# A gated linear recurrence and a gated MLP on one core: the recurrence cut into chunks of 64 tokens, its products as 64x64 blocks in four quadrants of TensorE

## The chip, the cores and the metric

The kernel runs on 1 core of one Trainium2 chip. The metric is the device time in microseconds (us) of one execution; lower is better. The engines of the core are named as in the profile: PE is TensorE (its weight loads are PEld), DVE is VectorE, ACT is ScalarE, POOL is GpSimd, SP is SyncE, which here issues all DMAs.

## What is computed

Two stages stand in a row. The first is a recurrence over 768 tokens for 4 sequences and 8 heads of 48 numbers, with a state of 48x48 per head that decays by a factor of its own for each token and row:

```python
for t in range(S):
    kt, vt, rt, wt = (k[:, :, t], v[:, :, t], r[:, :, t], w[:, :, t])
    cur = np.einsum('bhd,bhe->bhde', u[None] * kt, vt)
    y[:, :, t] = np.einsum('bhd,bhde->bhe', rt, state + cur)
    state = wt[:, :, :, None] * state + np.einsum('bhd,bhe->bhde', kt, vt)
```

The second takes y as x, 768 tokens of 384 numbers for each sequence:

```python
h = gelu_tanh(x @ w_in)                 # 384 -> 1024
u, v = h[..., :512], h[..., 512:]
v_n = (v - mean(v)) / sqrt(var(v) + 1e-6) * g_ln
v_s = einsum('ts,bsd->btd', w_sg, v_n) + b_sg    # over the tokens
out = x + (u * v_s) @ w_out             # 512 -> 384
```

## The kernel before

**The recurrence** is cut into steps of 128 tokens (`C`), 24 in all: 6 for each sequence. Heads stand in 4 pairs (`p`), one head of a pair in partitions 0 to 63 and the other in 64 to 127 (`j`). Within a step the recurrence becomes matrix products. A step has these parts, each a generator of its own:

- `decays` (line 403) makes running products of the decays with two scans on DVE (lines 408 and 413) and multiplies r by them (415); `decayed_k` does so for k (436).
- `own_weights` (439) makes one number per token and head, the term with `u`. For the first 8 steps (`OWN_PE`) PE sums it, with 4 matmuls of 8 columns (line 450); for the others three vector operations do (458, 460, 463). The numbers are put on the diagonal of two 128x512 blocks `a`, one for each `j`, by POOL (473) or by four ACT instructions (471).
- `scores` (477): 8 matmuls, one per head, give k against r over the step, 128x128 each (line 486, 64 rows of PE), and two `copy_predicated` (490) put what lies above the diagonal into `a`.
- `state` (492): 4 transposes of k (500), a copy, 8 matmuls with V (510), and an addition to the decayed state (520). `decayed` (522) multiplies the state by the decay of the step (531, 533). The last step of a sequence needs no new state and leaves this out.
- `outputs` (538): y is the product of the state with r (line 548, 8 matmuls; not in a sequence's first step) plus the product of `a` with V (line 563, 8 matmuls over 128 rows and 64 columns of PE). Three copies (267) carry y out of PSUM.

All these matmuls are float32. The profile lists two matmul records for each, and one for a transpose.

**The second stage** uses float32r operands split into a high and a low part, so that each product is three matmuls (lines 632, 633 and 634): `v_piece` (12 products of 512 columns for 128 tokens), `u_piece`, `gate_piece` and `out_piece` (products of 384 columns). They are called the dense matmuls here; there are 216 of 512 columns and 1152 of 384. x is split on PE for the first 6 steps (621, 622), later on DVE (627). Weights come as float64 bits and are turned into high and low parts on DVE and ACT; for `w_in` with PE's help (772, 773, 774).

**The order** is written ahead of the run by a planner (`Plan`). Each part yields operations with a cost on each engine that could do it, what it comes after and which buffers it takes; the planner keeps a clock for each engine, and where an operation may go on several engines it picks the one that ends it first. Ranks (`LEAD`, `FIRST`, `PIECE`, `WEIGHT`) say which stage goes first where two are ready. The instructions of each engine stand in the order that comes out; each engine keeps to it and waits at semaphores. The core's buffers for `a_ps` (2 banks for the scores), `k_ps` (transposed k, then the new state) and `y_ps` are one each in PSUM, and there are three `m_ps` for the second stage.

Of the kernel before, what the change touches and what calls it, by code (L numbers as in the profile page):

```python
# [12 lines left out]
U8 = mybir.dt.uint8  # L13
# [7 lines left out]
C = 128  # L21
NC = S // C
# [6 lines left out]
Q = C + 1  # L29
WL = NP * Q + 1  # L30
# [3 lines left out]
LEAD = (2.78, 2.05, 2.47, 2.9)  # L34
FIRST = {"v": -1.57, "u": 4.03, "gate": 5.24, "out": 7.56}
PIECE = {"v": -0.45, "u": 3.56, "gate": 5.0, "out": 7.56}
WEIGHT = {"v": -8.15, "u": -9.0, "sg0": 4.48, "sg1": 3.78, "out": 4.95, "g": -1.62}

OWN_PE = 8
COLD = 20.0  # L40
# [28 lines left out]
class Op:  # L69
# [3 lines left out]
    def __init__(self, on, after=(), take=(), free=(), done=None, kb=None, two=False):  # L73
        self.on, self.after, self.take, self.free, self.done, self.kb = on, after, take, free, done, kb
        self.two = two

# [29 lines left out]
class Slots:  # L106
# [5 lines left out]
    def since(self):  # L112
        return min(t for t, _ in self.free)
# [6 lines left out]
class Plan:  # L120
# [12 lines left out]
    @staticmethod  # L133
    def cost(e, c, t):
        return 2 * c if e == "PE" and t < COLD else c
# [13 lines left out]
    def run(self):  # L149
        while True:  # L150
            best = {}
            for p in self.procs:
# [3 lines left out]
                ready = max([p[2]] + [e.t for e in op.after] + [s.since() for s in op.take])  # L156
                t, c, e = min((s + self.cost(e, c, s), self.cost(e, c, s), e) for e, c in op.on.items()
                              for s in (max(ready, self.engines[e], self.port if op.port(e) else 0.0),))
                best.setdefault(e, []).append((t - c, p[0], p[4], p))
# [24 lines left out]
            p[2] = op.seen  # L184
# [75 lines left out]
def rwkv_gmlp(ctx: ExitStack, tc: tile.TileContext, wpad, kr, vtok, ktok, vt, u, w_in, g_ln, w_sgT, b_sg, w_out, out):  # L260
# [17 lines left out]
    ones = cp.tile([128, 128], F32, name="ones")  # L278
# [21 lines left out]
    s_w = slots("W", 2, [2 * 521])  # L300
# [18 lines left out]
    m_a = slots("a_ps", 1, [NP, C], [NP, C], at=ps)  # L319
# [6 lines left out]
    mask = per.tile([128, NP, C], U8, name="mask")  # L326
# [26 lines left out]
    plan.engines.update(DVE=2.0, POOL=3.0, ACT=2.1, SP=0.8)  # L353
# [23 lines left out]

    def load_kr(n):
# [3 lines left out]
        ch[n].kr.n = (g < NC - 1) + 1 + (g > 0)  # L382
# [3 lines left out]
    def load_v(n):  # L386
# [3 lines left out]
        ch[n].v.n = (g < NC - 1) + 1  # L390
# [9 lines left out]
    blocks = lambda t, o: t[:, o:o + NP * Q].rearrange("p (q x) -> p q x", x=Q)[:, :, 0:C]  # L400
    cols = lambda t: t.rearrange("p (q x) -> p q x", x=C)

    def decays(n):

        x = ch[n]
        yield Op({"DVE": 1.15}, after=[x.e_W], done=x.e_suf, two=True)
# [5 lines left out]
        yield Op({"DVE": 1.15}, done=x.e_pre, two=True)  # L412
# [5 lines left out]
    def range_check(n):  # L418
# [4 lines left out]
        both = x.w.tile.rearrange("p (a x) -> p a x", x=521)[:, :, 0:WL - 1]  # L423
        nc.scalar.activation(junk.rearrange("p (a x) -> p a x", a=2), both, AF.Square, accum_out=chk[:, n:n + 1])  # L424

    def chunk_pc(n):
        x = ch[n]
        op = yield Op({"ACT": 0.13, "POOL": 0.38}, after=[x.e_suf], take=[s_pc], done=x.e_pc)
        x.pc, = op.got
        x.w.done(op.seen)  # L430
        copy(op.e, x.pc.tile, x.Suf[:, 1:WL - 1:Q])
# [7 lines left out]
    def own_weights(n):  # L439

        x = ch[n]
        if n < OWN_PE:
# [4 lines left out]
            op = yield Op({"PE": 0.35}, after=[e_uc], take=[m_m], free=[rk])  # L447
# [16 lines left out]
        x.a = []  # L464
        for j in range(2):
            op = yield Op({"POOL": 0.95, "ACT": 1.2}, take=[s_a], done=(x.e_A0, x.e_A1)[j], free=[own] if j else [])
            x.a += op.got
            a = x.a[j].tile
            if op.e == "ACT":
                for p in range(NP):  # L470
                    nc.scalar.activation(a[:, p], ident, AF.Copy, scale=own.tile[:, 2 * p + j:2 * p + j + 1])  # L471
            else:
                nc.gpsimd.affine_select(a, own.tile[:, j:H:2].unsqueeze(2).broadcast_to([128, NP, C]),  # L473
# [594 lines left out]
```

## Time and profile before

| what | us |
|---|---|
| median of 3 runs (lowest, highest) | 403.65 (403.12, 405.01) |
| the profiled execution's own time | 402.04 |
| its span, first to last instruction | 400.3 |
| first PE instruction after the start | 6.39 |
| start of the last dense matmul | 393.51 |

The span is 1.74 us shorter than the profiled execution's time: this lies around the span. Durations in the profile are those of single instructions. Matmuls are pipelined, so that the busy time of one is longer than the distance from its start to the next start; what a group of matmuls costs on PE is read from the starts in the timeline. In a row of the timeline, "x16" is the number of records merged into it, "64\*64 64x128" the part of PE used (rows\*columns) and the moving operand. In a row of the windows, each engine has its busy time in that stretch and the number of its instructions that ran in it. The profile leaves out a few matmul records (1151 of 1152 are there).

### The profile page before, as it was taken

To read this page: it belongs to the slowest core of one execution; us is meant where nothing else is said; L and a number is where in the kernel's file an instruction comes from. 1 tells how busy PE (TensorE), PEld (TensorE's weight loads), DVE (VectorE), ACT (ScalarE), POOL (GpSimd) and SP (SyncE) were. 2 spreads that over 40 slices of the span, in tenths; PEclk is the share of its full clock that TensorE was granted. 3 is DMA by queue.
4 is the path that set the end of the run, shared out by engine and by line. 5 is a ranking of instruction groups with operands and counts; after the bars stand their busy time and mean duration, and the time that the engine had idled before them with its cause. 6 is when DMAs were issued, how large, how long until landed. Compare 5 with 4: busy or idle time off the path is not lost. (4 is left out here: it accounts for less than half of the span.)

```text
span 400.3 us, 7881 instructions
## 1 busy us (share of the span) xinstructions
PE 378.3 (95%) x2964; PEld 329.8 (82%) x2964; DVE 294.2 (73%) x573; ACT 200.2 (50%) x534; POOL 94.2 (24%) x127
## 2 busy tenths in 40 slices
PE   2799889999999999999999999999999999999993
PEld 2666567889898988988899988979899789999993
DVE  7699989889989999998798489956653355543251
ACT  3566575685555447746454246563272576502010
POOL 3003551123073543444550003124100002100000
PEclk9999899999999999999999999999999999999999
DMA  8918667343134634335422316222133520100101
GB/s 281 355 42 250 188 220 241 129 135 105 46 131 160 221 118 144 98 122 196 155 88 77 105 65 211 60 88 96 61 106 111 186 95 2 39 22 0 61 0 66
DMA packets 23933, 48.82 MB, mean 122 GB/s; under 512 B 4048, under 2 KB 13008, under 8 KB 23888
## 3 DMA queue, kind: packets, MB, share of 16 engines
q1 hardware_dynamic: 23888, 48.25, 36.6%
q8 instruction: 25, 0.41, 0.4%
q14 instruction: 20, 0.16, 0.1%
HBM read 42.34 MB, written 4.72 MB: 118 GB/s over the span
## 5 line engine op out<-in xcount | busy, mean ns | idle before, releaser
L632 PE MATMUL m_ps<-wsgh,vn 128*128 128x384 f32 x192 | 67.7, 353 | 0.8 <-DVE g L714 0.8
L634 PE MATMUL m_ps<-wsgh,vn 128*128 128x384 f32 x192 | 64.7, 337 | 0.0
L633 PE MATMUL m_ps<-wsgl,vn 128*128 128x384 f32 x192 | 64.6, 337 | 0.0
L473 POOL TENSOR_SCALAR_AFFINE_SELECT a<-own 128x512 f32<-128x512 f32 x25 | 20.3, 815 | 94.9 <-PE y_ps L563 44.9
L632 PEld LDWEIGHTS m_ps<-wsgh,vn 128*128 128x128 f32 x192 | 36.1, 188 | 5.5 <-issue 2.9
L712 ACT CAST g<-m_ps 128x384 fp32r<-128x384 f32 x32 | 15.1, 479 | 50.1 <-DVE m_ps L710 50.0
L490 DVE COPY_PREDICATED a<-mask,a_ps 128x512 f32<-128x512 uint8 x48 | 34.4, 730 | 4.5 <-POOL a L473 2.5
L663 POOL TENSOR_TENSOR st<-st,mhalf 128x1 f32<-128x1 f32 x24 | 15.3, 640 | 90.9 <-DVE st L661 87.7
L633 PEld LDWEIGHTS m_ps<-wsgl,vn 128*128 128x128 f32 x192 | 36.2, 188 | 0.4
L634 PEld LDWEIGHTS m_ps<-wsgh,vn 128*128 128x128 f32 x192 | 36.1, 188 | 0.0
L708 DVE SCALAR_TENSOR_TENSOR m_ps<-m_ps,g_ln,b_bc 128x384 f32<-128x384 f32 x32 | 19.7, 622 | 21.5 <-PE m_ps L634 21.4
L632 PE MATMUL m_ps<-g,wouth 128*128 128x384 f32 x96 | 33.7, 351 | 0.4 <-DVE g L714 0.4
L632 PE MATMUL m_ps<-xT,winh 128*128 128x384 f32 x96 | 33.4, 348 | 0.0
L408 DVE TENSOR_TENSOR_SCAN W<-W,D 128x516 f32<-128x516 f32 x24 | 32.0, 1332 | 1.6 <-DMA W<-in_wpad 1.6
L634 PE MATMUL m_ps<-xT,winl 128*128 128x384 f32 x96 | 32.4, 337 | 0.0
L633 PE MATMUL m_ps<-xT,winh 128*128 128x384 f32 x96 | 32.4, 337 | 0.0
L633 PE MATMUL m_ps<-g,wouth 128*128 128x384 f32 x96 | 32.4, 337 | 0.0
L634 PE MATMUL m_ps<-g,woutl 128*128 128x384 f32 x96 | 32.4, 337 | 0.0
L413 DVE TENSOR_TENSOR_SCAN W<-W,D 128x516 f32<-128x516 f32 x24 | 31.4, 1308 | 0.1
L471 ACT ACTIVATE a<-ident,own 128x128 f32<-128x128 f32 x92 | 29.1, 393 | 3.9 <-DVE own L463 3.8
L632 PE MATMUL m_ps<-winh,xT 128*128 128x512 f32 x72 | 30.5, 424 | 0.0
L424 ACT ACTIVATE junk<-W 128x1032 f32<-128x1032 f32 x24 | 25.6, 1066 | 9.8 <-DVE W L413 6.8
(142 smaller groups left out, 856.5 us busy)
## 6 DMA issues: line engine op xcount, KB each, us to landing
KR<-in_kr SPq DMA_DIRECT2D x24, 512.0 KB, 3.5
W<-in_wpad SPq DMA_DIRECT2D x24, 258.5 KB, 2.9
RK<-in_ktok SPq DMA_DIRECT2D x16, 384.0 KB, 3.2
vtok<-in_vtok SPq DMA_DIRECT2D x24, 192.0 KB, 3.1
out<-o SPq DMA_DIRECT2D x24, 192.0 KB, 1.9
KR<-in_w_in SPq DMA_DIRECT2D x6, 512.0 KB, 4.1
u<-in_w_sgT SPq DMA_DIRECT2D x12, 192.0 KB, 3.6
vn<-in_w_in SPq DMA_DIRECT2D x3, 512.0 KB, 7.3
```

Source lines behind the costliest of these rows:

```text
L408: nc.vector.tensor_tensor_scan(Suf[:, WL - 1:0:-1], W[:, WL - 1:0:-1], D1[:, WL - 1:0:-1], 0.0, ALU.mult, ALU.add)
L413: nc.vector.tensor_tensor_scan(W[:, 0:WL - 1], W[:, 0:WL - 1], D2[:, 0:WL - 1], 0.0, ALU.mult, ALU.add)
L424: nc.scalar.activation(junk.rearrange("p (a x) -> p a x", a=2), both, AF.Square, accum_out=chk[:, n:n + 1])
L471: nc.scalar.activation(a[:, p], ident, AF.Copy, scale=own.tile[:, 2 * p + j:2 * p + j + 1])
L473: nc.gpsimd.affine_select(a, own.tile[:, j:H:2].unsqueeze(2).broadcast_to([128, NP, C]), pattern=[[0, NP], [1, C]], compare_op=ALU.is_equa ...
L490: nc.vector.copy_predicated(x.a[j].tile, mask, a_ps.tile[j])
L632: nc.tensor.matmul(ps, lh, rh, start=(i == 0), stop=False)
L633: nc.tensor.matmul(ps, lh, rl, start=False, stop=False)
L634: nc.tensor.matmul(ps, ll, rh, start=False, stop=(i == n - 1))
L663: nc.gpsimd.tensor_tensor(rstd, var, c.mhalf, ALU.pow)
L708: nc.vector.scalar_tensor_tensor(ps, ps, c.g[:, d:d + 1], c.b_bc[:, ts], ALU.mult, ALU.add)
L712: nc.scalar.copy(gh, ps)
```

## The change

A step still covers 128 tokens, with the same loads, but inside it the recurrence goes in two chunks of 64 tokens (`T`):

- The decays get a mark at each 64 tokens (520 instead of 516 columns in the scans), and `chunk_pc` copies 8 decays instead of 4.
- `scores`: 16 matmuls of 64x64 (line 505), one for each head and chunk. Chunk `c_` of head `j` uses rows 64j and columns 64c_ of PE. The upper right block, second chunk against first, is no longer made, so that `a` is one 128x512 block with both chunks, and one `copy_predicated` (507) does what two did. `a` is filled from a diagonal of 64 by POOL, DVE (494) or 8 ACT instructions (492).
- `state`: the product with V is 16 matmuls (528), since each chunk has its own; they go to `a_ps` and not to `k_ps`. The state in the middle of a step is made (539), decayed (545, `T2`) and added to the second product (551). Now the last step of a sequence has this too, for its first chunk.
- `outputs` is in two parts. First 8 matmuls (580) of `a` with V, those in which rows and columns of PE lie crosswise; then `look`, a copy of one column of `y_ps` by ACT or DVE (592, printed as 282), and after it, in one group, the products of the two states with r (601, 8 or 16 matmuls) and the other 8 of `a` with V (580).
- `own` is summed on PE for 4 steps, not 8. `u_col` comes as one DMA, third on SP; before it came as two, the second of them 12th. The six DMAs of `move` are planned without a wait between them. The first loads have an order of their own.
- The planner's ranks and costs are other numbers, it has a small extra cost where a small matmul group begins, and a bias against DVE and POOL.

```diff
-OWN_PE = 8
-COLD = 20.0
+BIAS = {"DVE": 0.07, "POOL": 0.26}
+ON_PE = {"own": 4, "x": 6, "w": 6}
+COLD = 15.0
...
     def scores(n):
...
-        op = yield Op({"PE": 1.09}, after=[x.e_k, x.e_r], take=[m_a])
+        op = yield Op({"PE": 0.55}, small=True, after=[x.e_k, x.e_r], take=[m_a])
...
-        for p in range(NP):
-            for j in range(2):
-                nc.tensor.matmul(a_ps.tile[j][:, p], x.KR[64 * j:64 * j + 64, 0, p * C:(p + 1) * C],
-                                 x.KR[64 * j:64 * j + 64, 1, p * C:(p + 1) * C], start=True, stop=True)
-        for j in range(2):
-            yield Op({"DVE": 0.64}, after=[(x.e_A0, x.e_A1)[j]], free=[a_ps], done=(x.e_M0, x.e_M1)[j])
-            nc.vector.copy_predicated(x.a[j].tile, mask, a_ps.tile[j])
+        for p, j, c_ in [(p, j, c_) for p in range(NP) for j in range(2) for c_ in range(2)]:
+            k_, r_ = (x.KR[64 * j:64 * j + 64, i, p * C + c_ * T:p * C + c_ * T + T] for i in range(2))
+            nc.tensor.matmul(a_ps.tile[64 * c_:64 * c_ + 64, j, p * T:(p + 1) * T], k_, r_, start=True, stop=True)
+        yield Op({"DVE": 0.64}, after=[x.e_A], free=[a_ps], done=x.e_M)
+        nc.vector.copy_predicated(x.a.tile.rearrange("s j p t -> s j (p t)"), mask, a_ps.tile[:, :, 0:NP * T])
...
     def state(n):
...
-        for h in range(H):
-            j, p = h % 2, h // 2
-            nc.tensor.matmul(ds_ps[64 * j:64 * j + 64, p], kt.tile[:, p, 64 * j:64 * j + 64],
-                             x.V[:, h * D:(h + 1) * D], start=True, stop=True)
+        for p, c_, j in [(p, c_, j) for p in range(NP) for c_ in range(1 if last else 2) for j in range(2)]:
+            h = 2 * p + j
+            nc.tensor.matmul(ds.tile[64 * j:64 * j + 64, c_, p * 64:p * 64 + D],
+                             kt.tile[64 * c_:64 * c_ + 64, p, 64 * j:64 * j + 64],
+                             x.V[64 * c_:64 * c_ + 64, h * D:(h + 1) * D], start=True, stop=True)
...
+            nc.vector.tensor_tensor(mid, ds_ps[0], x.S2.tile[:, :, 0:D], ALU.add)
+        op = yield Op({"DVE": 0.3, "POOL": 0.6} if g else {"DVE": 0.3}, after=[x.e_pc], take=[s_S2], done=x.e_T2,
+                      free=[S1 if g else ds], two=g > 0)
...
+        engine[op.e].tensor_tensor(x.T2.tile[:, :, 0:D], mid,
+                                   x.pc.tile[:, :, 1].unsqueeze(2).broadcast_to([128, NP, D]), ALU.mult)
+        if not last:
...
+            nc.vector.tensor_tensor(x.S1.tile, ds_ps[1], x.T2.tile[:, :, 0:D], ALU.add)
...
     def outputs(n):
...
+        own_chunk([(q, c_, 1 - c_, r) for q in range(2) for c_ in range(2) for r in range(2)], True)
+        op = yield Op({"ACT": 0.2, "DVE": 0.1}, take=[s_look])
+        look, = op.got
+        copy(op.e, look.tile, y.tile[0][:, 1, C - 1:C])
...
+        for c_, S2 in enumerate((x.S2 if g else None, x.T2)):
...
+            for q, j, r in [(q, j, r) for q in range(2) for j in range(2) for r in range(2)]:
+                p = q + 2 * r
+                nc.tensor.matmul(place(j, q, r, c_), S2.tile[64 * j:64 * j + 64, p],
+                                 x.KR[64 * j:64 * j + 64, 1, p * C + c_ * T:p * C + c_ * T + T], start=False,
+                                 stop=(c_ != j), skip_group_check=True)
...
+        own_chunk([(q, c_, c_, r) for q in range(2) for c_ in range(2) for r in range(2)], False)
```

The order of the instructions is shown at three places. First PE at the first step of the second sequence, where y is made: `a` and `vtok` are its operands, `S` a state, `xT`, `winh`, `wsgh` and `vn` operands of dense matmuls. Before:

```order
L634 MATMUL m_ps_0_132<-xT_506,winl 128x384
L621 MATMUL m_ps_0_130<-x_0_106,ident 128x384
L622 MATMUL m_ps_0_130<-xT_811,minus 128x384
L563 MATMUL y_ps_0_128<-a_0_96,vtok_0_85 64x128 x4
L563 MATMUL y_ps_1_129<-a_0_97,vtok_0_85 64x128 x4
L632 MATMUL m_ps_0_130<-winh,xT_811 128x512
```

Now, from the last dense matmuls between the two parts of `outputs` on:

```order
L682 MATMUL m_ps_0_134<-wsgh,vn_1103 128x384
L680 MATMUL m_ps_0_133<-wsgh,vn_1103 128x384
L681 MATMUL m_ps_0_133<-wsgl,vn_1103 128x384
L682 MATMUL m_ps_0_133<-wsgh,vn_1103 128x384
L601 MATMUL y_ps_0_131<-KR_0_82,S_0_108 64x64 x2
L601 MATMUL y_ps_1_132<-KR_0_82,S_0_108 64x64 x2
L601 MATMUL y_ps_0_131<-KR_0_82,S_0_108 64x64 x2
L601 MATMUL y_ps_1_132<-KR_0_82,S_0_108 64x64 x2
L580 MATMUL y_ps_0_131<-a_0_98,vtok_0_85 64x64 x2
L580 MATMUL y_ps_1_132<-a_0_98,vtok_0_85 64x64 x2
L580 MATMUL y_ps_0_131<-a_0_98,vtok_0_85 64x64 x2
```

What stood in one group is in two, with dense matmuls between them, and a row is of 64 by 64. Counted over the program, the dense matmuls stand in 71 runs before and in 91 now, each run ending at small matmuls.

Second, PE around the first dense matmul of the program. Before, after the small matmuls of four steps:

```order
L621 MATMUL m_ps_0_132<-x_0_105,ident 128x384
L622 MATMUL m_ps_0_132<-xT_506,minus 128x384
L510 MATMUL k_ps_0_127<-vtok_0_85,kt_0_100 64x48 x8
L450 MATMUL m_ps_0_130<-u_col,RK_0_89 128x8 x4
L632 MATMUL m_ps_0_131<-winh,xT_506 128x512
```

Now, where the second step's scores have just been made (`KR_0_83`) and all six blocks of `w_in` are ready:

```order
L816 MATMUL m_ps_0_134<-winl,same 128x512
L669 MATMUL m_ps_0_135<-x_0_109,ident 128x384
L670 MATMUL m_ps_0_135<-xT_395,minus 128x384
L505 MATMUL a_ps_0_129<-KR_0_83 64x64 x16
L472 MATMUL m_ps_0_133<-u_col,RK_0_88 128x8 x4
L680 MATMUL m_ps_0_134<-winh,xT_395 128x512
L681 MATMUL m_ps_0_134<-winl,xT_395 128x512
```

The first dense matmul has moved from the fourth step to the second. Third, DVE at the second step, where the state is made. Before:

```order
L520 TENSOR_TENSOR S_0_102<-k_ps_0_127,S_0_103 128x192
L490 COPY_PREDICATED a_0_97<-mask,a_ps_0_125 128x512
L768 SCALAR_TENSOR_TENSOR winl<-xT_275 128x512
L267 CAST winl<-m_ps_0_131 128x512
L490 COPY_PREDICATED a_0_99<-mask,a_ps_1_126 128x512
```

Now:

```order
L539 TENSOR_TENSOR S_0_103<-a_ps_0_129,S_0_106 128x192
L810 SCALAR_TENSOR_TENSOR winl<-vn_320,vn_321 128x512
L545 TENSOR_TENSOR S_0_107<-S_0_103,pc_0_95 128x4x48
L429 SCALAR_TENSOR_TENSOR W_0_80<-W_0_80,D_136 128x520
L551 TENSOR_TENSOR S_0_104<-a_ps_0_129,S_0_107 128x192
L432 RECIPROCAL D_137<-W_0_80 128x8
L468 TENSOR_TENSOR RK_0_88<-KR_0_84 128x512
L434 SCALAR_TENSOR_TENSOR W_0_80<-W_0_80,D_137 128x520
L507 COPY_PREDICATED a_0_99<-mask,a_ps_0_129 128x512
```

One state operation on DVE has become three, with other work between them, and two masked copies have become one, which now comes behind the state.

More of the change, by code (lines that the diff above doesn't have):

```diff
@@ L69, with __init__ @@
 class Op:
[L73 removed]
+    def __init__(self, on, after=(), take=(), free=(), done=None, kb=None, two=False, apart=False, small=False):
         self.on, self.after, self.take, self.free, self.done, self.kb = on, after, take, free, done, kb
         self.two = two
+        self.small = small
+        self.apart = apart
     def port(self, e):
@@ L495, in state @@
         x = ch[n]
-        op = yield Op({"PE": 0.41}, after=[x.e_k], take=[m_s])
+        last = g == NC - 1
+        m = T if last else C
+        op = yield Op({"PE": 0.35}, small=True, after=[x.e_k], take=[m_s])
         kt_ps, = op.got
@@ L550, in outputs, with own_chunk @@
+        def own_chunk(order, start):
+            for q, c_, j, r in order:
+                p = q + 2 * r
+                h = 2 * p + j
+                nc.tensor.matmul(place(j, q, r, c_), x.V[64 * c_:64 * c_ + 64, h * D:h * D + 64],
+                                 x.a.tile[64 * c_:64 * c_ + 64, j, p], start=(start and q == 0), stop=not start,
                                  skip_group_check=True)
-            x.S2.done(op.seen)
-            x.kr.done(op.seen)
-        op = yield Op({"PE": 1.03}, after=[x.e_M0, x.e_M1, x.e_V, *([] if g else turn)],
-                      take=[] if g else [m_y], done=x.e_ym)
+        op = yield Op({"PE": 0.33}, small=True, after=[x.e_M, x.e_V, *turn], take=[m_y])
@@ L568, in outputs @@
         y0, y1 = (t[:, :, 0:C] for t in y.tile)
-        op = yield Op({"ACT": 0.19, "DVE": 0.22}, take=[s_y3] if first else [])
+        y.n = 3
+        op = yield Op({"ACT": 0.3, "DVE": 0.35}, take=[s_x] if first else [], free=[y], apart=True)
+        seen = op.seen
+        if first:
+            half.x, = op.got
+            half.x.n = KT + 3
+        copy(op.e, half.x.tile[:, 0:2, cs], y0)
+        op = yield Op({"ACT": 0.19, "DVE": 0.22}, free=[y], apart=True)
+        seen = max(seen, op.seen)
+        copy(op.e, half.x.tile[:, 2, cs], y1[:, 0])
+        op = yield Op({"ACT": 0.19, "DVE": 0.22}, take=[s_y3] if first else [], free=[y], apart=True)
         if first:
@@ L572, in outputs @@
         copy(op.e, half.y3.tile[:, cs], y1[:, 1])
-        op = yield Op({"ACT": 0.19, "DVE": 0.22}, take=[s_x] if first else [])
-        if first:
-            half.x, = op.got
-            half.x.n = KT + 3
-        copy(op.e, half.x.tile[:, 2, cs], y1[:, 0])
-        op = yield Op({"ACT": 0.3, "DVE": 0.35}, free=[y], done=x.e_y)
-        copy(op.e, half.x.tile[:, 0:2, cs], y0)
+        x.e_y.t = max(seen, op.seen)
     halves = {}
```

284 lines of the change are left out of this document (148 added, 136 removed).

## The prediction

> **What bounds the kernel now.** I read the windows of each engine first, to see which engine is full in which stretch, then the waits of PE, then the timeline of PE at places where small matmul groups stand between dense ones, and last DVE. The columns of the windows are the stretch in us, its length, busy time and instructions of PE, PEld, DVE, ACT and POOL, PE's granted clock, the DMA share and GB/s.
>
> ```profile
> 0.00:20.00 20.00, 10.58 (x57) 8.61 (x58) 13.80 (x25) 9.58 (x26) 3.78 (x20) 1.00 0.86 318
> 20.00:40.00 20.00, 18.88 (x195) 13.22 (x194) 20.00 (x36) 13.56 (x41) 3.64 (x4) 1.00 0.48 146
> 40.00:60.00 20.00, 16.88 (x165) 11.80 (x163) 18.07 (x27) 13.05 (x41) 10.38 (x13) 0.91 0.64 204
> 60.00:140.00 80.00, 79.36 (x679) 69.06 (x681) 72.80 (x143) 46.70 (x125) 26.08 (x28) 1.00 0.46 146
> 140.00:220.00 80.00, 79.53 (x667) 69.21 (x664) 72.17 (x135) 44.50 (x118) 31.48 (x36) 1.00 0.38 125
> 220.00:300.00 80.00, 80.00 (x655) 69.98 (x656) 55.33 (x117) 38.80 (x103) 14.27 (x20) 1.00 0.30 99
> 300.00:380.00 80.00, 79.63 (x489) 75.12 (x486) 34.35 (x81) 32.12 (x83) 4.58 (x8) 1.00 0.20 65
> ```
>
> From 60 to 380 us PE is busy 318.5 of 320 us. What is taken out of its queue there moves the end by as much, if nothing else comes to be waited for. Before 60 us it isn't PE: it is idle 13.7 us, and DVE is full from 20 to 40. DVE stays over 90% to 220 and then falls away. Busy times of DVE overlap a little, so 90% is less than full, but the reserve is small. DMA is no bound after the start. The waits of PE say the same: they are few and early.
>
> ```profile
> PE k_ps L500 <- DVE KR L436: 6.4, 1, 6.4
> PE m_ps L450 <- DMA u_col<-in_u: 2.4, 1, 2.4
> PE m_ps L632 <- DVE g L714: 1.3, 3, 0.5
> ```
>
> So the sum is made over PE's queue, from start to start, with one term for the first 60 us.
>
> **What a small group costs.** Two stretches of PE's timeline hold one group of each kind (start, duration, then line, names, part of PE used, moving operand, records):
>
> ```profile
> 222.94 0.34 PE L633 MATMUL m_ps<-wsgl,vn 128*128 128x384 f32 x1
> 223.12 0.34 PE L634 MATMUL m_ps<-wsgh,vn 128*128 128x384 f32 x1
> 223.39 0.67 PE L548 MATMUL y_ps<-KR,S 64*64 64x128 f32 x16
> 223.98 0.44 PE L632 MATMUL m_ps<-wsgh,vn 128*128 128x384 f32 x1
> 224.26 0.34 PE L633 MATMUL m_ps<-wsgl,vn 128*128 128x384 f32 x1
> 224.44 0.34 PE L634 MATMUL m_ps<-wsgh,vn 128*128 128x384 f32 x1
> 224.71 1.09 PE L563 MATMUL y_ps<-a,vtok 128*64 128x128 f32 x16
> 225.73 0.44 PE L632 MATMUL m_ps<-wsgh,vn 128*128 128x384 f32 x1
> ```
>
> ```profile
> 164.22 0.60 PE L500 MATMUL k_ps<-ident,KR 128*128 128x128 f32 x4
> 164.75 1.16 PE L486 MATMUL a_ps<-KR 64*128 64x128 f32 x16
> 165.84 0.67 PE L510 MATMUL k_ps<-vtok,kt 128*64 128x48 f32 x16
> 166.44 0.44 PE L632 MATMUL m_ps<-g,wouth 128*128 128x384 f32 x1
> ```
>
> From start to start: transposes 0.53, scores 1.09, state 0.60, product of the state 0.59, product with V 1.02. How often each stands there follows from its records in the groups, 16 (4 for transposes) each:
>
> ```profile
> L486 PE MATMUL a_ps<-KR 64*128 64x128 f32 x384 | 29.7, 298 | 0.8 <-DVE KR L436 0.8
> L563 PE MATMUL y_ps<-a,vtok 128*64 128x128 f32 x384 | 26.5, 279 | 0.1
> L510 PE MATMUL k_ps<-vtok,kt 128*64 128x48 f32 x320 | 13.9, 231 | 0.7 <-ACT kt L267 0.7
> L548 PE MATMUL y_ps<-KR,S 64*64 64x128 f32 x320 | 13.8, 282 | 2.0 <-ACT S L531 2.0
> L500 PE MATMUL k_ps<-ident,KR 128*128 128x128 f32 x80 | 12.9, 286 | 6.4 <-DVE KR L436 6.4
> ```
>
> Before: 24 x 1.09 + 24 x 1.02 + 20 x 0.59 + 20 x 0.60 + 20 x 0.53 = 26.2 + 24.5 + 11.8 + 12.0 + 10.6 = **85.1 us**.
>
> For the price of the new groups I need what one round costs, a round being the records that run side by side, one in each part of PE. That quadrants do run side by side is seen in the windows of L548 alone (PE, then PEld, with the records that ran in each stretch):
>
> ```profile
> 223.38:223.42 0.04, 0.03 (x4) 0.04 (x4) 1.00 0.25 77
> 223.42:223.50 0.08, 0.08 (x4) 0.08 (x8) 1.00 0.09 19
> 223.50:223.60 0.10, 0.10 (x8) 0.10 (x12) 1.00 0.00 0
> ```
>
> Four matmuls have started by 0.03 us after the first, no fifth by 0.11, and four more by 0.21. So L548 is 4 rounds of four, and L563, which uses two halves of the columns, 8 rounds of two. With 128 moving columns in both, 4R + f = 0.59 and 8R + f = 1.02 give R = 0.108 for a round and f = 0.16 for the beginning and end of a group. L510 is 8 rounds as well, with weights of 64 columns and 48 moving columns: 8r + 0.16 = 0.60, r = 0.055. A new round has weights of 64 columns and 48 or 64 moving columns. Half of R would be 0.054; I take 0.058, next to L510, and keep 0.054 and 0.108 (nothing won by halving the columns) as ends.
>
> By a rule of the Trainium skill, "TensorE: Matmul & The Clock Gate", section "Back-to-back issue gap", two matmuls never start less than about 25 ns apart, however few columns they have. An estimate from it is 0.100 us for a round of four; the 752 rounds of the sum below would cost 75 us by it and 44 us by the price from the trace. The trace disagrees for the first four of a group, which started within 30 ns together; it has no run of rounds as short as the new ones in four quadrants.
>
> **The sum.** All in us, start to start, on PE's queue:
> - Scores: 16 matmuls, 32 records, 8 rounds: 8 x 0.058 + 0.16 = 0.62, 24 times, 14.9.
> - State: 8 rounds, 0.62, 14.9 for 24 (the last step of a sequence has half the matmuls, but in two quadrants).
> - First part of y: 4 rounds, 0.39, 9.4 for 24.
> - Second part: 12 rounds, 0.86, 20 times, and 8 rounds, 0.62, 4 times: 19.7.
> - Transposes: 24 x 0.53 = 12.7.
>
> Now 71.6 instead of 85.1: **-13.5**. These are 752 rounds in all, so that each nanosecond of a round weighs 0.75 us.
>
> Entering a small group from dense matmuls costs 0.27 - 0.18 = 0.09 (223.12 to 223.39, against 222.94 to 223.12), coming back 0.28 - 0.18 = 0.10 (223.98 to 224.26, against the next). Runs of dense matmuls go from 71 to 91: 20 x 0.19 = **+3.8**. Against that, 13 groups of the 64x64 shape now directly follow another of that shape, where the end of a group may not cost its 0.09: **-1.2** (between 0 and -2.1, all of f).
>
> The own terms leave PE for four steps:
>
> ```profile
> 67.43 0.95 PE L450 MATMUL m_ps<-u_col,RK 128*128 128x8 f32 x8
> 68.24 0.48 PE L632 MATMUL m_ps<-winh,xT 128*128 128x512 f32 x1
> ```
>
> 4 x 0.81 = **-3.2**. Their three vector operations a step go to POOL and DVE.
>
> The first 60 us: PE waits 2.36 for the second `u_col` DMA, and from this come the own weights, `a`, and a stop of DVE:
>
> ```profile
> 13.63 3.55 PE L450 MATMUL m_ps<-u_col,RK 128*128 128x8 f32 x16 [2.36 <-DMA u_col<-in_u]
> 18.65 0.73 DVE L490 COPY_PREDICATED a<-mask,a_ps 128x512 f32<-128x512 uint8 x1 [2.47 <-POOL a L473]
> 49.55 0.48 PE L632 MATMUL m_ps<-winh,xT 128*128 128x512 f32 x1
> ```
>
> Third on SP, the DMA comes with the first loads, and DVE, the bound there, gets about 2.4 us back: **-2.4**. The first dense matmul (49.55 now) comes earlier by two steps; I count nothing for that, since what PE does early in dense work it must do later in small groups, while DVE sets the pace. Ends: -6 if PE really is filled better, +4 if the new order runs into DMAs or into the single `a_ps`, which scores and state now share.
>
> At no cost I put the rest. `look` makes the second part of y wait for a copy; PE has dense or other matmuls of 0.5 us or more between the parts. A hand-over of that kind takes 0.68 with a copy of 512 columns (rows below), and `look` copies one. Its cover is gone where the copying engine is late: queued behind PE's wait are then all dense matmuls.
>
> ```profile
> 6.39 1.08 PE L500 MATMUL k_ps<-ident,KR 128*128 128x128 f32 x4 [6.39 <-DVE KR L436]
> 8.15 1.10 PE L510 MATMUL k_ps<-vtok,kt 128*64 128x48 f32 x16 [0.68 <-ACT kt L267]
> ```
>
> Moved DMAs of `move` only shift on SP, which has few by then.
>
> Together -13.5 + 3.8 - 1.2 - 3.2 - 2.4 = -16.5. The profiled execution, 402.04, becomes 385.5; the median of the runs stands 1.6 above it, so 403.65 - 16.5 = **387**. With the ends of the small terms this case reaches from 382 to 392.
>
> **Rivals.**
> *DVE takes over.* Two rows with the next start give its prices:
>
> ```profile
> 29.62 0.34 DVE L520 TENSOR_TENSOR S<-k_ps,S 128x192 f32<-128x192 f32 x1
> 29.88 0.74 DVE L490 COPY_PREDICATED a<-mask,a_ps 128x512 f32<-128x512 uint8 x1
> 30.51 1.44 DVE L768 SCALAR_TENSOR_TENSOR winl<-xT 128x512 fp32r<-128x512 uint32 x1
> ```
>
> 24 masked copies go (-24 x 0.63 = -15), but 24 additions and 26 products of the state come (+50 x 0.26 = +13), 11 fillings of `a` of 512 columns (0.63 each, like the masked copy, +7), 11 looks, and operations that POOL or PE had; I count +7 net. Behind each stands PE with scores, state and both parts of y. If all 7 reach the end: 394, and with more hand-overs late, 399. For it: DVE is over 90% to 220. Against it: from 220 on it has 25 us free in each 80, and little of the second stage hangs on the newest step.
>
> *PE filled from the start.* If the early dense work takes the idle time, up to 5 us more go: 382, down to 378.
>
> *Rounds that don't shorten.* The gain is gone where a round costs 0.058 + 16.5/752 = 0.080; beyond it the change loses. At R = 0.108 the time is 387 + 752 x 0.050 = 425. By the Trainium skill's 25 ns between starts it would be 419, an estimate. The place is every group of the recurrence. For it speaks that no row shows four quadrants at 64 columns, where PE has to take 8 instructions, loads and matmuls, in 58 ns; against it L510's round and the four starts in 30 ns.
>
> *It doesn't do what it says:* if only two of four quadrants ran side by side, rounds would be twice as many: +752 x 0.058, 431. L548 speaks against it.
>
> **Chances.** Forecast 0.66, DVE 0.17, filled start 0.10, long rounds 0.05, pairs 0.02. A measurement here can tell about 0.5%, 2 us, from no change. Faster: 0.66 + 0.10 + 0.12 of the DVE case = 0.88. The rest of that case gives 0.04 to no change and 0.01 to slower, and with the last two slower is 0.08. The range leaves out the slow ones, the worst of the DVE case and the best of the start: 380 to 398.
>
> **What would show it.** In the profile after: groups of scores (32 records) 0.62 from start to start, first part of y 0.39, second 0.86. A second part longer than 1.5, or scores of 1.0, would make the prediction wrong by the rounds. PE's waits between 60 and 360 should stay under 5 us; if waits on DVE (masked copies, `S`) or on `look` stand there with 10 us, DVE has taken over. The wait for `u_col` should be gone, and DVE's stop at the first masked copy shorter. The first dense matmul should stand near 30.

## The result, and the profile after

The changed kernel takes 393.25 us (median of 4 runs, 393.03 to 395.35), the kernel before 404.19 (4 runs beside it, 403.12 to 405.01): a ratio of 0.974 with a 95% interval of 0.970 to 0.979. That is 10.9 us less (10.4 by the ratio); 16.5 were forecast, and the 387 of the forecast lies 6 us below the measured time, the range of 380 to 398 around it. Ratios here and below leave out an execution that took over 1.5% longer than the fastest of the same kernel. The profiled execution took 393.27 with a span of 391.5, 8.8 us less than the one before.

The windows of each engine after, with the columns of the prediction:

```profile
0.00:20.00 20.00, 12.69 (x146) 9.36 (x147) 17.30 (x33) 9.68 (x26) 7.47 (x24) 1.00 0.88 295
20.00:40.00 20.00, 18.21 (x328) 12.72 (x326) 19.44 (x44) 17.22 (x55) 1.93 (x2) 0.91 0.49 157
40.00:60.00 20.00, 14.21 (x181) 10.04 (x181) 13.45 (x28) 11.03 (x31) 1.73 (x2) 0.91 0.76 236
60.00:140.00 80.00, 73.46 (x1037) 63.02 (x1038) 75.94 (x151) 47.00 (x136) 19.04 (x20) 1.00 0.48 151
140.00:220.00 80.00, 80.00 (x1210) 69.14 (x1209) 75.73 (x157) 54.67 (x154) 20.05 (x23) 1.00 0.45 142
220.00:300.00 80.00, 79.52 (x1022) 70.76 (x1025) 54.31 (x121) 37.21 (x95) 9.80 (x11) 1.00 0.29 96
300.00:380.00 80.00, 79.27 (x558) 74.27 (x548) 37.30 (x91) 33.36 (x83) 4.42 (x8) 1.00 0.19 64
```

From 140 us on PE is as full as before. From 60 to 140 it now stands 6.5 us of 80, where it stood 0.6, and in the first 60 us 14.9, where it stood 13.7. The line of busy times on the two pages, first after and then before, splits the 8.8 us:

```profile
PE 362.3 (93%) x4484; PEld 314.0 (80%) x4484; DVE 295.7 (76%) x625; ACT 210.6 (54%) x577; POOL 64.4 (16%) x90
```

```profile
PE 378.3 (95%) x2964; PEld 329.8 (82%) x2964; DVE 294.2 (73%) x573; ACT 200.2 (50%) x534; POOL 94.2 (24%) x127
```

PE's busy time shrank by 16.0, and the time in which it does nothing grew from 400.3 - 378.3 = 22.0 to 391.5 - 362.3 = 29.2, by 7.2; together -8.8. DVE's busy time grew by 1.5. All 1152 dense matmuls of 384 columns are in both profiles. The new groups of small matmuls cost what was summed. PE's timeline shows the first dense matmul, at 30.25 where it stood at 49.55, then the two parts of y in the second step, and scores later on (distances from start to start: 0.39, then 0.86, then 0.62):

```profile
30.25 0.48 PE L680 MATMUL m_ps<-winh,xT 128*128 128x512 f32 x1
...
31.12 0.46 PE L580 MATMUL y_ps<-a,vtok 64*64 64x64 f32 x16
31.51 0.50 PE L680 MATMUL m_ps<-winh,xT 128*128 128x512 f32 x1
...
32.41 0.69 PE L601 MATMUL y_ps<-KR,S 64*64 64x64 f32 x32
...
33.27 0.50 PE L680 MATMUL m_ps<-winh,xT 128*128 128x512 f32 x1
...
306.21 0.69 PE L505 MATMUL a_ps<-KR 64*64 64x64 f32 x32
306.83 0.44 PE L680 MATMUL m_ps<-wsgh,vn 128*128 128x384 f32 x1
```

From the waits of PE after (us in total, times, longest): the first is the wait at the start, 6.4 before; the wait for `u_col` is gone, and others stand in its place, for S, for a DMA and for ACT.

```profile
PE m_ps L472 <- DVE RK L468: 5.8, 1, 5.8
PE a_ps L505 <- DVE S L551: 3.1, 1, 3.1
PE m_ps L669 <- DMA x<-y: 2.0, 1, 2.0
PE a_ps L528 <- issue: 1.9, 1, 1.9
...
PE m_ps L680 <- ACT u L736: 1.7, 1, 1.7
```

The longest of them behind the start, in the timelines of ACT, DVE and PE around 60 us: DVE stands at a low part of `w_sg` (L848), whose high part, made on ACT, waits for its load; the addition to the state (L551) is queued behind it, and the scores on PE wait for that, because state and scores now share `a_ps`:

```profile
59.76 0.51 ACT L282 CAST wsgh<-u 128x384 fp32r<-128x384 f32 x1 [2.01 <-DMA u<-in_w_sgT]
```

```profile
60.30 0.56 DVE L848 TENSOR_TENSOR wsgl<-u,wsgh 128x384 fp32r<-128x384 f32 x1 [2.27 <-ACT wsgh L282]
...
60.96 0.35 DVE L551 TENSOR_TENSOR S<-a_ps,S 128x192 f32<-128x192 f32 x1
```

```profile
61.37 0.69 PE L505 MATMUL a_ps<-KR 64*64 64x64 f32 x32 [3.10 <-DVE S L551]
```

This wait is not of the same size in each execution: in dve_late and light_out below, which have the same instructions up to there, it is 2.4 and 1.5.

From 80 to 100 us the waits go through ACT's queue to DVE. ACT stands 1.92 us for one number per row that DVE makes late (L713), and `u`, for which PE waits, is queued on ACT behind that:

```profile
93.44 0.81 ACT L716 ACTIVATE v<-v,st 128x512 f32<-128x512 f32 x1 [1.92 <-DVE st L713]
...
95.03 0.49 ACT L736 ACTIVATE u<-m_ps 128x384 f32<-128x384 f32 x1
```

```profile
95.58 0.44 PE L680 MATMUL m_ps<-xT,winh 128*128 128x384 f32 x1 [1.69 <-ACT u L736]
```

### The profile page after: what moved, and what is told of

The parts are those of the page before. It is cut to its first block, busy times and chain, and to the rows that moved or that the text cites. A ratio compares the mean times of both kernels' runs of the same rounds, so it can differ in the third digit from the quotient of the medians.

```text
span 391.5 us, 10972 instructions
## 1 busy us (share of the span) xinstructions
PE 362.3 (93%) x4484; PEld 314.0 (80%) x4484; DVE 295.7 (76%) x625; ACT 210.6 (54%) x577; POOL 64.4 (16%) x90
## 4 chain that ended last, share of the span: by engine, by line
PE 78%; DVE 7%; DMA 6%; ACT 3%; POOL 2%; issue 2%; ACTq 0%; DVEq 0%; POOLq 0%
PE m_ps L680 23%; PE m_ps L682 19%; PE m_ps L681 19%; PE a_ps L505 3%; PE y_ps L580 3%; PE y_ps L601 3%; PE a_ps L528 3%; DMA u<-in_w_sgT 2%; PE k_ps L519 2%; DMA vtok<-in_vtok 2%; DMA KR<-in_kr 2%; PE m_ps L814 1%; ACT a L492 1%; DVE m_ps L756 1%; PE m_ps L669 1%
## 5 line engine op out<-in xcount | busy, mean ns | idle before, releaser
L445 ACT ACTIVATE junk<-W 128x1040 f32<-128x1040 f32 x24 | 25.7, 1072 | 14.6 <-DVE W L434 7.3
L680 PE MATMUL m_ps<-winh,xT 128*128 128x512 f32 x72 | 31.3, 435 | 0.5 <-DVE g L762 0.5
L429 DVE TENSOR_TENSOR_SCAN W<-W,D 128x520 f32<-128x520 f32 x24 | 29.5, 1231 | 1.5 <-DMA W<-in_wpad 1.5
L434 DVE TENSOR_TENSOR_SCAN W<-W,D 128x520 f32<-128x520 f32 x24 | 30.0, 1251 | 0.1
L682 PE MATMUL m_ps<-winh,xT 128*128 128x512 f32 x72 | 28.7, 398 | 0.4 <-ACT xT L282 0.4
L681 PE MATMUL m_ps<-winl,xT 128*128 128x512 f32 x72 | 28.7, 399 | 0.0
L736 ACT ACTIVATE u<-m_ps 128x384 f32<-128x384 f32 x32 | 15.7, 489 | 22.8 <-PE m_ps L682 22.6
```

Of the source, the lines that this page charges most:

```text
L429: nc.vector.tensor_tensor_scan(Suf[:, WL - 1:0:-1], W[:, WL - 1:0:-1], D1[:, WL - 1:0:-1], 0.0, ALU.mult, ALU.add)
L434: nc.vector.tensor_tensor_scan(W[:, 0:WL - 1], W[:, 0:WL - 1], D2[:, 0:WL - 1], 0.0, ALU.mult, ALU.add)
L680: nc.tensor.matmul(ps, lh, rh, start=(i == 0), stop=False)
L681: nc.tensor.matmul(ps, lh, rl, start=False, stop=False)
L682: nc.tensor.matmul(ps, ll, rh, start=False, stop=(i == n - 1))
L736: nc.scalar.activation(h_.u[f].tile, ps, AF.Gelu_apprx_tanh)
```

## The experiments

Two theories stood at the start. **A:** the small groups gave what was summed, and 6 to 9 us were given back between 36 and 115 us, because the loads of `w_sg` come late in the new order and DVE stands in line at them. **B**, the prediction's rival: DVE's work is itself the bound there. A difference to the changed kernel is given as (ratio - 0.9743) x 404; the intervals of the two ratios make about 2 us of it uncertain.

| run | ratio to before (95%) | us against the changed kernel | PE busy | PE not busy |
|---|---|---|---|---|
| changed kernel | 0.974 (0.970 to 0.979) | | 362.3 | 29.2 |
| small_sg | 0.973 (0.969 to 0.976) | -0.7 | 365.1 | 27.1 |
| light_state | 0.969 (0.966 to 0.972) | -2.1 | 362.6 | 25.0 |
| scores_twice | 0.997 (0.994 to 1.000) | +9.2 | 374.4 | 26.9 |
| sg_ranks | 1.010 (1.006 to 1.013) | +14.4 | 365.1 | 39.3 |
| one_quadrant | 1.014 (1.007 to 1.020) | +15.9 | 388.6 | 26.6 |
| old_tables | 1.008 (1.005 to 1.012) | +13.6 | 368.3 | 38.1 |
| pool_moves | 0.970 (0.967 to 0.973) | -1.7 | 362.7 | 27.6 |
| sg_early | 1.025 (1.021 to 1.029) | +20.3 | 370.1 | 39.1 |
| dve_early | 0.986 (0.983 to 0.989) | +4.6 | 366.4 | 29.6 |
| dve_late | 0.978 (0.972 to 0.983) | +1.4 | 362.4 | 30.2 |
| light_out | 0.970 (0.966 to 0.973) | -1.9 | 361.4 | 28.4 |
| before_ucol | 0.984 (0.980 to 0.987) | (-6.6 against before) | 376.5 | 20.8 |

The last two columns are of the profiled executions, one for each kernel: busy time from the page, and the span less that. PE's busy time also grows where its clock is lower. The profiled execution of one_quadrant took 417.02, its three others 409.68 to 414.23, so that its row is too high in them.

### What the small groups cost

**scores_twice.**

```diff
-        for p, j, c_ in [(p, j, c_) for p in range(NP) for j in range(2) for c_ in range(2)]:
+        for p, j, c_ in [(p, j, c_) for p in range(NP) for j in range(2) for c_ in range(2)] * 2:
```

> Each group of scores is sent twice (the second pass writes the same numbers over the first): 8 more rounds in each of 24 groups. At the 0.058 us that a round was given, a group grows from 0.62 to 1.08 and PE's path by 24 x 0.46 = 11. Theory A (PE's path sets the end nearly everywhere): 403 to 405. Theory B (DVE sets the pace to 220 us): only the groups behind that count in full, 397 to 400.

```profile
303.58 1.16 PE L505 MATMUL a_ps<-KR 64*64 64x64 f32 x64
304.67 0.44 PE L680 MATMUL m_ps<-wsgh,vn 128*128 128x384 f32 x1
```

A group takes 1.09 (304.67 - 303.58) instead of 0.62, so a round is 0.47 / 8 = 0.059. PE's busy time grew by 12.1, near 24 x 0.47 = 11.3, and the time by 9.2 (median 402.85, just below the 403 to 405 of A and well above the range of B): most of what is added to PE's queue reaches the end.

**one_quadrant.**

```diff
-        for p, j, c_ in [(p, j, c_) for p in range(NP) for j in range(2) for c_ in range(2)]:
+        for p, j, c_ in [(p, j, c_) for j in range(2) for c_ in range(2) for p in range(NP)]:
```

> The 16 products of each group of scores are sent quadrant by quadrant (four pairs of heads in one quadrant, then the next) instead of round by round; the same numbers. If a round of 0.058 us is the time that one quadrant is busy, and four share it only because neighbours in the queue fall in different quadrants, a group takes 16 x 0.058 + 0.16 = 1.1 instead of 0.62, and the kernel 393 + 24 x 0.46 = 404. If the round is set by the sending of its instructions, nothing changes: 0.62 and 393.

```profile
329.13 1.54 PE L505 MATMUL a_ps<-KR 64*64 64x64 f32 x32
330.60 0.44 PE L680 MATMUL m_ps<-wsgh,vn 128*128 128x384 f32 x1
```

The group takes 1.47 instead of 0.62, where 1.1 was expected. The expectation counted 16 products, but each has two records, 32 in a group. In the trace their starts form four chains of 8, read here as the four quadrants: 58 ns apart within a chain behind its second start, and each chain begins about 0.29 after the one before, while three records of that are still to come. So 0.058 is the time that one record of 64 columns keeps its quadrant; sent quadrant by quadrant, only the end of one chain runs beside the beginning of the next, and four run side by side only when neighbours in the queue lie in different quadrants. 24 x 0.85 = 20.4 more on PE, 15.9 in the time, with about 3 us of uncertainty. The order of the three loops is thus worth more here than the whole change brought.

### Where the stops of 36 to 62 us come from

**small_sg.**

```diff
-        nc.sync.dma_start(raw.tile, src)
+        nc.sync.dma_start(raw.tile[:, 0:16], src[:, 0:16])
+        wide = raw.tile[:, 0:16].unsqueeze(1).broadcast_to([128, 24, 16])
```

> Same instructions in the same order, but each of the 12 loads of w_sg moves 16 of its 384 columns, and its high and low parts are made from these 16 repeated (so most of w_sg is left out of the result). Theory A (the small groups gave what was summed, and some 6 to 9 us were given back between 36 and 115 us because DVE stands in line behind the low parts of w_sg, whose loads come late): DVE's stop at the low parts and PE's wait for S behind them go, 386 to 389 instead of 393.3. Theory B (DVE's added work is itself the bound from 40 to 140 us): DVE has as much to do as before, 392 to 394.

The kernel leaves out most of `w_sg`. No difference (393.52). The wait of the scores for S fell from 3.1 to 0.6, as A had it, and another took its place: the longest wait for x grew from 2.0 to 3.5, at the x of the third step. Its six small copies (`x<-y`) stand on SP behind the loads of RK, KR and V, and they land only at 50.8. SP's timeline and PE's:

```profile
41.18 0.38 SPq L419 DMA_DIRECT2D RK<-in_ktok  x1
41.65 0.38 SPq L405 DMA_DIRECT2D KR<-in_kr  x1
42.12 0.38 SPq L413 DMA_DIRECT2D vtok<-in_vtok  x1
42.60 4.58 SPq L648 DMA_DIRECT2D x<-y  x6
```

```profile
50.85 1.65 PE L669 MATMUL m_ps<-x,ident 128*128 128x384 f32 x2 [3.51 <-DMA x<-y]
```

Over the whole profiled execution PE's idle time fell by 2.1, and its busy time rose by 2.8 at a lower clock (0.83 from 40 to 60 us, 0.91 in the changed kernel). So the bytes of `w_sg` are not what holds the time up, and A in this form falls: taking one stop away shows the next.

**pool_moves.**

```diff
+                q = nc.gpsimd if h_.n < 6 else nc.sync
-                nc.sync.dma_start(x[64 * j + D:64 * j + 64, i, ts], y3[64 * j + 16 * i:64 * j + 16 * i + 16, ts])
+                q.dma_start(x[64 * j + D:64 * j + 64, i, ts], y3[64 * j + 16 * i:64 * j + 16 * i + 16, ts])
```

> The 36 small copies of y into x of the first batch are issued from GpSimd's queue, which is nearly idle there, instead of SyncE's; the order on the other engines is the same. Theory A, as left by the run with little of w_sg moved (SyncE's line and the loads bunched behind it, not the bytes of w_sg, make PE wait for x and S from 36 to 62 us): the loads behind the copies go out 3 to 4 us sooner and the wait for x shrinks: 388 to 391. Theory B (DVE's work is the bound): 392 to 394. If GpSimd needs 1 us or more for each issue, rstd of the first pieces comes late behind them, and it is slower than 394.

393.24, and -1.7 by the ratio, within the uncertainty: inconclusive. PE's wait for S behind 58 us is down to 0.6, one of 1.9 for x stays, and a new one of 1.9 for DVE is in the list of its waits. An issue takes POOL 0.52 us (36 in 18.3).

### What another order costs

**sg_ranks** sets three ranks back, **old_tables** all four tables, **sg_early** lets `w_sg` come earlier; in each the order is planned anew.

```diff
-WEIGHT = {"v": -8.23, "u": -3.71, "sg0": 3.28, "sg1": -0.95, "out": 3.69, "g": 4.15}
+WEIGHT = {"v": -8.23, "u": -3.71, "sg0": 4.48, "sg1": 3.78, "out": 4.95, "g": 4.15}
```

> The changed kernel with three ranks of the table of weights as they were before the change (sg0 4.48, sg1 3.78, out 4.95), and the order planned with them: the loads of w_sg stand later on SP, and their low parts behind S and the masked copies on DVE. Theory A: the stop of 6 us between 51 and 61 us goes, 387 to 390, or less gain if the first gate pieces then wait for w_sg. Theory B: as much for DVE to do, 392 to 394.

```diff
+LEAD = (2.78, 2.05, 2.47, 2.9)
+FIRST = {"v": -1.57, "u": 4.03, "gate": 5.24, "out": 7.56}
+PIECE = {"v": -0.45, "u": 3.56, "gate": 5.0, "out": 7.56}
+WEIGHT = {"v": -8.15, "u": -9.0, "sg0": 4.48, "sg1": 3.78, "out": 4.95, "g": -1.62}
```

> The changed kernel with all four tables of ranks (LEAD, FIRST, PIECE, WEIGHT) as before the change, the order planned with them. Theory A (the arithmetic carries the gain, the new order is worth little or cost something): 388 to 397. Rival (the new order carries a share as large as the small groups): 398 to 406, with PE's waits up by 5 to 13 us.

```diff
-            plan.add(WEIGHT[f"sg{i}"] + 0.1 * s, f32_weight(*w[1:], e_wsg[s, i], [ch[2 + 2 * i].e_k]))
+            plan.add(WEIGHT[f"sg{i}"] + 0.1 * s, f32_weight(*w[1:], e_wsg[s, i], [ch[1].e_k]))
```

> The planner may load w_sg from step 1 on (it was step 2 for the first half, 4 for the second): seven or eight of the twelve loads then stand on SyncE ahead of the load of W that waits 6 us for its slot at 25 to 32 us, while the DMA engines are nearly idle; the order is planned anew with it. Theory A: the bunch of 36 to 62 us is thinner, 388 to 391. Theory B: as much for DVE to do and its low parts come earlier still, 392 to 396.

All three came out slower than the kernel before, at 408.49, 408.08 and 414.92, with the same small groups, and outside every range that was expected. Nearest was the rival in old_tables, that the order carries as much as the groups (398 to 406, PE's waits up by 5 to 13). PE's idle time is 9 to 10 us above that of the changed kernel in each, and its busy time 2.8 to 7.8 above, with the same matmuls; switches between small and dense matmuls are fewer, by 1 to 6. The planner also gave DVE 3.9 to 6.2 us more to do, and ACT and POOL less, so that these runs price the order together with the placing of the work. The profile of old_tables shows what PE's idle and busy time are made of. Its waits, in the timeline of PE:

```profile
132.74 1.14 PE L505 MATMUL a_ps<-KR 64*64 64x64 f32 x32 [4.00 <-DVE S L551]
136.51 1.06 PE L519 MATMUL k_ps<-ident,KR 128*64 128x128 f32 x4 [2.63 <-DVE KR L458]
```

and what DVE does ahead of L551, for which the scores wait 4.00:

```profile
128.47 1.23 DVE L434 TENSOR_TENSOR_SCAN W<-W,D 128x520 f32<-128x520 f32 x1
...
130.33 0.69 DVE L436 TENSOR_TENSOR KR<-KR,W 128x512 f32<-128x512 f32 x1
132.06 0.36 DVE L802 TENSOR_SCALAR g<-g 128x384 int32<-128x384 int32 x1 [1.04 <-DMA g<-in_w_out]
132.34 0.35 DVE L551 TENSOR_TENSOR S<-a_ps,S 128x192 f32<-128x192 f32 x1
```

It is the mechanism of 60 us in the changed kernel again: DVE is full, a weight that waits for its DMA stands ahead of S, and the single `a_ps` carries this to the scores and so to all of PE. The waits cost twice, since PE's granted clock falls behind them. Over the executions behind the ratios its mean is 0.968 in sg_ranks, 0.969 in old_tables and 0.955 in sg_early, against 0.981 in the changed kernel. In old_tables (columns PE, PEld, DVE, ACT, POOL, clock):

```profile
129.10:132.50 3.40, 0.00 (x0) 0.00 (x0) 2.36 (x6) 1.86 (x4) 0.99 (x1) 0.99 0.92 296
132.50:135.90 3.40, 1.14 (x32) 0.95 (x32) 3.08 (x8) 1.83 (x6) 0.00 (x0) 0.50 0.73 280
...
139.30:142.70 3.40, 3.40 (x12) 3.40 (x12) 2.54 (x7) 1.17 (x6) 0.00 (x0) 0.51 0.58 214
142.70:146.10 3.40, 3.40 (x22) 3.40 (x21) 3.40 (x8) 1.71 (x5) 0.00 (x0) 1.00 0.18 63
```

### What DVE's work costs

**light_state** narrows the state's products and additions, here the second addition:

```diff
-            nc.vector.tensor_tensor(x.S1.tile, ds_ps[1], x.T2.tile[:, :, 0:D], ALU.add)
+            nc.vector.tensor_tensor(x.S1.tile[:, 0:1], ds_ps[1][:, 0:1], x.T2.tile[:, 0:1, 0:D], ALU.add)
```

> Same order, but DVE's, POOL's and ACT's products and additions of the state treat one pair of heads of the four (48 columns of 192), the other three pairs of the state stay zero (left out of the result). Some 84 instructions become shorter by about 0.13 us, 11 us together, nearly all on DVE. Theory A: the stop at the low parts of w_sg stays, only the catching up behind it is quicker, 390 to 393. Theory B: DVE's work is the bound, 385 to 388.

The kernel leaves out three of the four pairs of heads in the state. 391.46, where A had put it, and not B; the -2.1 of the ratio is hardly clear of the uncertainty. DVE's busy time fell by 8.5 (295.7 to 287.2) over the whole run. Its longest stop at the low parts of `w_sg` stays, at 2.2, but PE's wait for S behind it is gone: whether such a stop reaches PE depends on what DVE has in line behind it.

**dve_early** and **dve_late**, with `n >= 14` in place of `n < 10`:

```diff
+        for _ in range(2 if n < 10 else 1):
+            nc.vector.copy_predicated(x.a.tile.rearrange("s j p t -> s j (p t)"), mask, a_ps.tile[:, :, 0:NP * T])
```

> The masked copy of the scores is made twice in the first 10 of 24 steps (the second writes the same numbers): 10 x 0.62 = 6.2 us more on DVE before 135 us, the order and the planner's costs unchanged. Theory B as it now stands (DVE is the bound of the first 140 us and has slack behind; with 8.5 us less on DVE in the run with a light state, some 3 to 4 of them before 140 us, 1.8 to 3.9 were won): 397 to 400. Theory C (PE's waits come from single stops, at DMAs and in lines, whatever DVE's load): 393 to 395.

> The same doubling in the last 10 steps, behind 165 us: 6.2 us more on DVE. Theory B: nothing, 392.5 to 394.5, since DVE has 25 us free in each 80 from 220 us on. If DVE's line, not its load, decides (each instruction ahead of a hand-over counts): 396 to 400.

Early, 6.2 us more of DVE cost 4.6 (398.81), as B expected: 0.7 for each, 0.4 to 1.1 with both intervals. Late they cost 1.4, between -1.5 and +4.3 with both intervals: three of five runs stood at 394.3 to 394.6, one at 399.1, and one at 400.9 that the ratio leaves out, so that it doesn't settle it. In the two profiled executions the early price shows as lowered clock: PE's busy time grew by 4.1 and its idle time by 0.4, and the clock over the first 60 us is 0.89 (below) instead of 0.94. But over all executions the mean clock is 0.980 against 0.981, so that lowered clock doesn't explain the price in general.

```profile
0.00:60.00 60.00, 45.49 (x645) 32.13 (x645) 52.01 (x106) 37.33 (x106) 9.93 (x28) 0.89 0.67 218
```

**light_out** leaves out four operations of `f64_weight` where it makes `w_out`, here one:

```diff
-        nc.vector.tensor_scalar(f.bitcast(I32), t, -0x800000, None, ALU.bitwise_and)
+        if on_pe:
+            nc.vector.tensor_scalar(f.bitcast(I32), t, -0x800000, None, ALU.bitwise_and)
```

> Four of the six operations that take each piece of w_out apart are left out (the weights come out wrong): 4 x 1.7 = 6.7 us less on DVE, all of it between 70 and 93 us, the order otherwise the same. Theory B: 386 to 389, and PE's waits of 80 to 100 us (4.6 us, through ACT's line) mostly gone. Theory C: 392 to 394.

392.07, at the low edge of C and far from B, and -1.9 by the ratio, for 5.6 us less on DVE (295.7 to 290.1). Of PE's wait for `u` 1.0 us is left of 1.7, the others of 80 to 100 us stand; the wait for S at 60 us is shorter too, but nothing was left out ahead of it. So DVE's work early on costs about 0.7 us for each that is added, but where it is taken away at most about a third comes back, in two runs each of which is hardly clear of no change. That other stops of nearly the same size stand behind is the reading that fits, and the waits that stay support it. DVE is one bound of the first 140 us, beside the line on SP and the hand-overs, and not the only one.

### The start alone

**before_ucol**, the kernel before with one part of the change:

```diff
-            nc.sync.dma_start(u_col.rearrange("p a b -> p (a b)")[64 * j:64 * j + D, j:NP * H:10],
-                              u.rearrange("(p j) d -> j d p", j=2)[j])
+        nc.sync.dma_start(u_col, ucol)
...
-    plan.add(-8.0, columns())
+    plan.add(-8.9, columns())
```

> The kernel before with one part of the change: u_col comes laid out in one DMA, third on SyncE, instead of by two strided ones behind it; nothing else. The prediction gave this 2.4 us (PE's wait of 2.36 and DVE's stop of 2.47 at the first masked copy): 401 to 402.5. Rival: the start is bound by the loads of w_in and DVE's work on them anyway: 403.5 to 405.

398.05 against 404.92, a gain of 6.6 by the ratio (5.1 to 8.1), far beyond both expectations. The planner moved other instructions with it: PE's own terms now stand first. Its windows show PE and DVE fuller in the first 20 us (11.57 and 15.57, they were 10.58 and 13.80), and no fall of the clock from 40 to 60:

```profile
0.00:20.00 20.00, 11.57 (x59) 9.05 (x60) 15.57 (x27) 9.48 (x25) 5.48 (x20) 1.00 0.85 305
...
40.00:60.00 20.00, 17.63 (x189) 12.52 (x187) 16.74 (x34) 15.03 (x41) 8.86 (x10) 1.00 0.81 253
```

The two profiled executions differ by 2.9 only; how the rest of the 6.6 is made up is not settled.

Set beside the changed kernel, this run says what the rest of the change is worth: from a ratio of 0.984 to 0.974, some 4 us, 1.5 to 6 with both intervals. By the profiled executions PE's busy time falls from 376.5 to 362.3 between the two, by 14.2, and its idle time grows from 20.8 to 29.2, by 8.4. That the parts of the change simply add is taken for granted here; no run shows the chunks without `u_col`.

## Why the prediction was right in sign and range, and 6 us too low

- **The price of the groups: right.** Scores 0.62, parts of y 0.39 and 0.86, round 0.059 for 0.058. The rival of rounds that don't shorten is refuted: its 0.080, 0.100 and 0.108 all lie far above. one_quadrant shows what long groups would have taken: neighbours in one quadrant.
- **PE's sum: right, a little short.** Groups, runs, neighbours and own terms were -13.5 + 3.8 - 1.2 - 3.2 = -14.1; PE's busy time fell by 16.0, with 3.4 us more of lowered clock in it (0.91 in two windows of 20 us, before in one). Busy time and distances from start to start are not the same measure, so the two agree only roughly.
- **The first 60 us: wrong.** -2.4 was forecast for the wait for `u_col`. It went, and so did DVE's stop at the first masked copy, but PE is idle 1.2 us longer there: a longer wait for x (2.0), waits for `a` (1.8) and for kt (1.1), and a stop inside a group (1.9) took its place. Alone, this part of the change is worth more than I gave it (6.6 in the kernel before). I counted nothing for the first dense matmul coming earlier, and it did, by 19 us; PE's queue was not fuller for it.
- **"At no cost I put the rest": this is the step that failed.** "PE's waits between 60 and 360 should stay under 5 us" was its test, and PE is idle 6.5 us from 60 to 140 alone, where it was idle 0.6. The 5.9 us between the two and the 3.6 of the start (2.4 to be saved, 1.2 lost) make 9.5; PE's busy time, 1.9 below the sum, gives a part back, and the forecast (-16.5) is 7.7 away from the profiled executions (-8.8). What I had named as a small end of the start's term, the single `a_ps` that scores and state share, carries the longest of these waits; S is late because DVE, full or standing at a weight, is late.
- **The rival "DVE takes over" was half of the truth.** Its price, 394, is nearer to the 393.25 than the forecast, but by luck: it stood on 7 us more work for DVE, and DVE's busy time grew by 1.5. The time went into hand-overs that came late. The rival holds up to 140 us, where each us more on DVE cost about 0.7; from 140 to 220 DVE is as full (75.7 of 80) and PE stands nowhere. The forecast's argument, that little of the second stage hangs on the newest step, holds there, and in the first 140 us it does not. That the second stage has no stock of work yet in those is the likely reason, argued and not shown.
- **The order: not weighed.** I moved the first dense matmul at no cost and gave the order an end of +4. Three other orders of the same operations are 14 to 20 us slower, with some work placed elsewhere too, so that this term had the widest range of all. That it came out well here I had no row for: that the measured time lies inside the range is in this part luck.

## What to carry to other kernels

Where one engine is full, a sum over its queue tells well what leaves that queue (here 14.1 summed, 16.0 less busy); what the sum leaves out is whether its feeders keep up, and that is read stage by stage: DVE, at 91% from 60 to 140 before the change, had too little room there for late hand-overs, and at 95% from 140 to 220 after it, it kept PE waiting nowhere. If two producers come to share one buffer, ask which late consumer now holds up the other. And a change that plans the order anew needs a range for the order of its own, from other orders of the same operations, before its small terms are worth adding up.

## What of the hardware was not expected

**The clock can fall behind a stretch that is half idle.** In both kernels PE's clock was 0.5 for stretches of 3.4 us, and no wait had to last that long first. After (the columns as above):

```profile
39.40:42.80 3.40, 1.50 (x35) 1.03 (x29) 2.27 (x7) 1.92 (x5) 0.00 (x0) 0.99 0.52 135
42.80:46.20 3.40, 3.40 (x11) 2.57 (x10) 3.40 (x7) 2.39 (x5) 0.00 (x0) 0.51 0.93 343
```

PE was busy 1.50 of 3.4 us, with a longest stop of 1.9, and then ran at half speed for the next 3.4, at a cost of up to 1.7. The Trainium skill, "TensorE: Matmul & The Clock Gate", section "What's actually happening", gives the two states and the window of about 3.4 us, and the slow one after at least one idle window; the trace agrees with the states and the window, but a window less than half busy was enough. The busy share alone doesn't decide: in the same profile the clock stayed at 1.00 behind a window busy for 1.73 of 3.4 (93.9 to 97.3) and fell to 0.51 behind one busy for 2.33 (18.9 to 22.3), with small matmuls in it.

**PE stops inside a group with no wait to name.** In the middle of the state's 32 records PE stood 1.90 us ("issue"; 20 records, then 12). From 38 to 43 us the view of the DMA queues shows one packet of 0.02 MB on the instruction queue q8, whose packets over the run go with PE's records: 25 before for 2964, 37 now for 4484, and 43 in scores_twice for 5252.

```profile
39.21 0.55 PE L528 MATMUL a_ps<-vtok,kt 64*64 64x48 f32 x20
41.66 0.43 PE L528 MATMUL a_ps<-vtok,kt 64*64 64x48 f32 x12 [1.90 <-issue]
```

That the code came late is argued, not shown. In scores_twice, where the same group runs through, PE then waits 1.4 for x at the same place, so that the stop itself costs little here; but it is the longest idle stretch of the window above, behind which the clock fell.

**POOL and DVE hold each other up.** While POOL multiplied two tensors, a DVE addition that took 0.55 at another place took 1.23:

```profile
91.85 1.01 POOL L482 TENSOR_TENSOR RK<-RK 128x384 f32<-128x384 f32 x1
```

```profile
77.30 0.55 DVE L823 TENSOR_TENSOR woutl<-g 128x384 fp32r<-128x384 f32 x1
...
92.04 1.23 DVE L823 TENSOR_TENSOR woutl<-g 128x384 fp32r<-128x384 f32 x1
```

At 158.9 it was POOL that was held up: its product (L480) took 1.53, where the median of twelve is 1.02, and DVE's beside it (L436) kept its 0.68. Work that is moved from DVE to POOL is therefore not simply gone from DVE.
